# An MoE slot's layer 2 moved behind the next slot's layer 1, fetches without branches, late slots in two branches, weight regions at 64-byte multiples

## The chip, the core and the metric

The kernel runs on one core of a Trainium2 chip. The metric is the device time of one execution in microseconds; lower is better. Each kernel is executed several times and the median is given; one more execution is recorded by the hardware profiler, and all rows below come from that one.

## What is computed

A causal attention with a memory term, followed by a mixture of experts in which each token goes to its best expert. The reference, cut to what matters:

```python
# q, k, v: 4 batches, 8 heads, 576 positions, 64 columns, float32
a = softmax(causal(q @ k.T / 8));  local = a @ v
q_p = phi(q)                              # phi(x) = x + 1 for x > 0, exp(x) otherwise
mem = (q_p @ M_prev) / (q_p @ z_prev + 1e-6)
x = g * mem + (1 - g) * local             # g = 1 / (1 + exp(-beta)); then 2304 rows of 512
logits = normalised(x) @ normalised(expert_emb).T / tau      # 8 experts
e = argmax(logits);  gate = softmax(logits)[e]
for each expert e:                        # w1[e]: 512 x 1024, w2[e]: 1024 x 512
    out[rows of e] = gate * (relu(x @ w1[e]) @ w2[e])
```

## The kernel before

Until about 257 us the kernel computes the attention, then each token's expert; from then on the experts. The order of the first part is made by a small planner (`Sched`, lines 40 to 164): each operation has an engine, an assumed duration, dependencies and a priority, and the planner issues them by these. The table `PRIO` (line 37) holds the priorities' offsets; other numbers in it give another order of the same operations.

The expert stage works in slots of 128 rows, all of one expert. Three early slots, -3 to -1, belong to the expert with the most tokens and are planned together with the end of the attention (`early_slots`, line 1565). The main slots 0 to 24 follow in plainly written order (`l1`, `l2`, `first`, `second`, `rest`, from line 1645). Slots 0 to 14 always run (`NFIX` is 15). Each later one stands in a branch on a flag that the kernel computes (`when`, line 1636), nested in that of the slot before. With this data the slots 0 to 18 have rows, so slots 15 to 18 run inside branches, and 19 is the first that is skipped.

A slot's steps are:

- `off_reg`, `load_ids`, `gather`, `gather_g`: SyncE reads the slot's start from a table and loads its row numbers; GpSimd fetches the rows (L1422) and their gates (L1429) by indirect DMA. `x_T` is a transposing DMA on SyncE's queue (L1464) into one of two buffers `xT`; `x_hi` on ScalarE (L1468) and `x_lo` on VectorE (L1471) move its two halves to one of two places in `xhl`.
- Layer 1 (L1478): 4 chunks of 6 matmuls with 512 columns, three products of high and low parts for each half of the output, into two PSUM banks. `e_relu` (ScalarE, L1487) makes `hs`.
- `e_T` (L1491): 8 transposes of `hs` on TensorE. `e_hi` (ScalarE, L1495) and `e_lo` (VectorE, L1499) split the result into `hhl`.
- Layer 2 (L1505): 8 chunks of 3 matmuls with 512 columns. For a main slot `y_out` (VectorE, L1511) multiplies by the gate; for an early one `y_copy` (L1517) and a product on GpSimd (L1522) do that. `y_store` is an indirect DMA of GpSimd (L1529).

The weights come in fp32 into `RA` by DMA (L1340, L1342 for the early prefetch, L1351, L1354 later). Where a slot starts a new expert, `split_if` (L1437 is its branch) makes high and low parts on ScalarE (L1369) and VectorE (L1373), for layer 1 in `RB` and for layer 2 in `RC`. The matmuls of both layers read their 512 moving columns from `RB` and `RC`.

In the main stage the layers of neighbouring slots are woven together: half of layer 1 of slot i+1, its other half, half of layer 2 of slot i, the transposes of slot i+1, the other half of layer 2. Slot -1 isn't woven in: its layer 2 is finished in the early stage, before slot 0's layer 1. Slot 1's layer 1 takes slot 0's transposes in its middle (`if i == 1 and c == 1` in `l1`). In a branch each engine that takes part loads the flag and jumps for itself, and at the end of a branch not taken it makes up for the signals that it left out.

`pause` (line 226) is a tile of one element, allocated ahead of `RA`, `RB` and `RC`; in the built program these start at bytes 17,312, 50,080 and 82,848 of each partition, which is 32 bytes behind a multiple of 64.

Of the kernel before, what the change touches and what calls it, by code (L numbers as in the profile page):

```python
# [36 lines left out]
PRIO = {'po': {'S': -6.056184646814478, 'M': -5.666575449467843, 'E': 0.3840305535611125, 'T': -2.8418202194000335, 'H': -2.7510329935167688, 'L': -4.504325722743113, 'C': -0.7444419325520046}, 'pa': 0.08970844558892392, 'pv': -1.5671314454708472, 'sq': -14.84720101963438, 'xt': 2, 'ra': 0, 'aD': 1, 'ps': 1.7384297857956093, 'lv': 23.82858121560453, 'pr': 2.0466758035936374, 'rs': 0, 'w1p': 130.2350106796488, 'ag': 0, 'pb': 9.186065914959338, 'lqk': -2.2845849071912188, 'rr': 2, 'aA': 1, 'pe4': 2, 'ep': 143.81283877036086, 'w2p': 208.68596613061786, 'slack': 40.00092317974874, 'pp': 1.1250262799121031, 'fc': (1, 2), 'nw2l': 2, 'nw1l': 4, 'xlo': 1, 'wpd': 2, 'w1': 300000, 'ND': 2, 'avl': 2, 'ph': 1, 'avc': 1, 'phat': -11148.311932377628, 'ae': 1, 'rp': 0}  # L37
# [130 lines left out]
def kernel(  # L168
# [57 lines left out]
    pause = cst.tile([1, 1], F32, name="pause")  # L226
    gate_dram = dr.tile([NTOK + P, 1], F32, name="gate_dram")

# [3 lines left out]
    RC = cst.tile([P, 8192], F32R, name="RC")  # L232
    QK = [
# [1160 lines left out]
    G = {}  # L1394
# [153 lines left out]
    def early_slots():  # L1548
# [5 lines left out]
        for which in (1, 2):  # L1554
            for c in range(4):
                op(("wpf", which, c), "SP", 450,
                   lambda which=which, c=c: w_dma1(which, c, regs[-1]["nx"], cond=regs[-1]["pf"]),
                   (("wpr",), (f"w{which}l", c)) + ((), (("eix", 1),), (("exT", 0),), (("exT", 1),))[cfg.get("wpd", 2)], p0 + which, xfer=1456)
# [5 lines left out]
        for i in range(-NEARLY, 1):  # L1564
            pp = p0 + 10 * (i + NEARLY)
            old = i - 2 >= -NEARLY
            op(("exT", i), "SP", 1175, lambda i=i: x_T(i), (("eg", i),) + ((("gst",),) if i == 0 else ()) + ((("exs", i - 2), ("exl", i - 2)) if old else ()), pp, xfer=896)
            op(("exs", i), "ACT", c_act(512), lambda i=i: x_hi(i), (("exT", i),) + ((("el1", i - 2, KD - 1),) if old else ()), pp)
# [3 lines left out]
            for c in range(KD):  # L1572
                def f(i=i, c=c):
# [14 lines left out]
            op(("egg", i), "POOL", 1040, lambda i=i: gather_g(i), (("gst",), ("eix", i)), pp + 6, xfer=56, late=3500)  # L1588
            for c in range(KF):
                def f(i=i, c=c):  # L1590
                    if c == 0:
                        G[i]["yp"] = bank(("ey", i), "L" if i < -1 else "aux")
                    l2c(i, c)
                op(("el2", i, c), "PE", 3 * 236, f,
                   (("ehl", i, c // 4), ("w2l", c // 2)) + ((("el2", i, c - 1),) if c else ()), pp + 5,
                   alloc=() if c else (("L", ("ey", i)),) if i < -1 else (("aux", ("ey", i), 0, 3),))
# [45 lines left out]
    def maybe(i, engines):  # L1642
        return nullcontext() if i <= NFIX else when(i, engines)

    def l1(i):

        G[i]["hp"] = [pbank((2 if i == 1 else 0) + n) for n in range(2)]
        more = i + 1 < NSLOT
        for c in range(KD):
            l1c(i, c)  # L1650
            if i == 1 and c == 1:
                for n in range(2):
                    e_T(0, n, pbank(n))
                    e_hi(0, n)
                    e_lo(0, n)
        if more and i:
# [124 lines left out]
```

## Time and profile before

| | us |
|---|---|
| median of 3 runs | 556.67 |
| lowest and highest of them | 555.46 and 559.15 |
| the profiled execution | 553.01 |
| its span in the trace | 551.2 |

The mean granted clock of TensorE is 0.99 of its full speed in the profiled execution. Times in the rows count from the start of the span; the profiled execution's own time is 1.8 us longer than the span. PE is TensorE's matmuls, PEld its weight loads, which run beside them, DVE is VectorE, ACT ScalarE, POOL GpSimd and SP SyncE; a "q" behind a name is that engine's instruction queue, and a DMA that an engine issues stands under it. In rows of a timeline the first two numbers are the start and the duration, from the first instruction of the group to the end of the last; ends of matmuls are modelled and reach into the next group, so the pace is read from start to start. The square brackets give the idle time ahead of a group and what ended it.

### The profile page before, as it was taken

What the parts mean: (1) busy time and instruction counts of PE and PEld (TensorE: products, weight loads), DVE (VectorE), ACT (ScalarE), POOL (GpSimd) and SP (SyncE); (2) the same over time, 40 slices, a digit from 0 to 9 for tenths busy, and PEclk for the clock granted to TensorE, in tenths of its full rate; (3) what the DMA queues carried; (4) which work ended last, traced back from release to release, by engine and by line L of the source; (5) the groups of instructions that cost most, each with busy time, mean ns of one, the idle gap of its engine ahead of it and who ended that gap; (6) DMA issues with size and microseconds to landing.
All of it is one profiled execution on the core that took longest, in us unless ns stands there. A gap on an engine that the chain in (4) does not pass through costs nothing. (4 is left out here: it accounts for less than half of the span.)

```text
span 551.2 us, 11278 instructions
## 1 busy us (share of the span) xinstructions
PE 522.2 (95%) x3489; PEld 439.8 (80%) x3489; DVE 319.6 (58%) x1019; ACT 301.5 (55%) x592; POOL 226.3 (41%) x284
## 2 busy tenths in 40 slices
PE   7999999899999999998898899999999999999990
PEld 6788988798898989887686688888888888888870
DVE  5687777687777777789951133521267515664440
ACT  5777867676776867786322243422256525653340
POOL 6152573748446763777534322122232322212200
PEclk9999999999999999999999999999999999999996
DMA  6667744234643330579139636652268864774100
GB/s 156 138 82 161 178 92 117 48 73 108 156 91 45 77 65 14 124 246 168 39 66 357 110 75 232 161 96 58 59 211 278 222 170 122 245 235 156 39 15 21
DMA packets 124428, 70.33 MB, mean 128 GB/s; under 512 B 108600, under 2 KB 108728, under 8 KB 124354
## 3 DMA queue, kind: packets, MB, share of 16 engines
q1 hardware_dynamic: 119554, 58.96, 43.5%
q0 software_dynamic: 4800, 10.52, 6.7%
q8 instruction: 30, 0.49, 0.4%
q14 instruction: 44, 0.36, 0.2%
HBM read 110.69 MB, written 10.67 MB: 220 GB/s over the span
## 5 line engine op out<-in xcount | busy, mean ns | idle before, releaser
L1478 PE MATMUL aux<-RB,xhl 128*128 128x512 f32 x528 | 129.1, 398 | 2.8 <-ACTq L1437 2.8
L1505 PE MATMUL L<-RC,hhl 128*128 128x512 f32 x504 | 125.9, 399 | 0.3 <-ACT RC L1369 0.3
L1478 PEld LDWEIGHTS aux<-RB,xhl 128*128 128x128 f32 x528 | 98.8, 189 | 27.1 <-ACTq L1437 3.6
L1505 PEld LDWEIGHTS L<-RC,hhl 128*128 128x128 f32 x504 | 93.2, 188 | 21.9 <-issue 0.7
L1499 DVE TENSOR_TENSOR hhl<-aux,hhl 128x512 fp32r<-128x512 f32 x44 | 30.1, 689 | 117.0 <-ACT hhl L1495 54.7
L746 PE MATMUL L<-VN,aT 128*128 128x128 f32 x640 | 87.0, 276 | 0.0
L1529 POOL DMA_INDIRECT out_dram<-ys,ix x22 | 22.8, 1036 | 144.6 <-DVE ys L1511 130.1
L746 PEld LDWEIGHTS L<-VN,aT 128*128 128x128 f32 x640 | 78.4, 192 | 1.4 <-issue 0.6
L682 DVE CUSTOM_DVE_ANT_0 a<-aux,mask 128x128 f32<-128x128 f32 (+3 forms) x144 | 61.9, 452 | 14.0 <-PE aux L671 9.9
L1495 ACT ACTIVATE hhl<-aux 128x512 fp32r<-128x512 f32 x44 | 25.8, 595 | 74.2 <-PE aux L1491 43.9
L710 ACT ACTIVATE a<-a,nb 128x128 f32<-128x128 f32 (+3 forms) x128 | 65.1, 557 | 0.7 <-issue 0.2
L719 PE MATMUL aux<-ident,a 128*128 128x128 f32 x384 | 62.6, 280 | 1.6 <-ACT a L712 1.5
L731 ACT ACTIVATE aT<-aux 128x512 f32<-128x512 f32 (+3 forms) x83 | 42.4, 518 | 27.6 <-PE aux L719 26.2
L1487 ACT ACTIVATE hs<-aux 128x512 f32<-128x512 f32 x44 | 24.0, 595 | 55.4 <-PE aux L1478 55.1
L719 PEld LDWEIGHTS aux<-ident,a 128*128 128x128 f32 x384 | 42.7, 141 | 12.9 <-issue 4.0
L899 POOL TENSOR_TENSOR A<-ms,dd 128x256 f32<-128x256 f32 x32 | 20.5, 642 | 67.0 <-DVE dd L883 17.1
L1422 POOL DMA_INDIRECT a<-x_dram,ix x22 | 23.1, 1050 | 38.4 <-DMA ix<-id_dram 18.2
L1373 DVE TENSOR_TENSOR RB<-RA,RB 128x1024 fp32r<-128x1024 f32 x24 | 29.3, 1225 | 10.2 <-ACT RB L1369 10.2
L733 DVE COPY aT<-aux 128x512 f32<-128x512 f32 (+3 forms) x45 | 23.8, 530 | 12.4 <-PE aux L719 8.9
L649 POOL TENSOR_SCALAR RA<-RA 128x576 f32<-128x576 f32 x14 | 23.3, 1662 | 15.8 <-ACT RA L570 15.8
L1369 ACT ACTIVATE RB<-RA 128x1024 fp32r<-128x1024 f32 x24 | 25.4, 1061 | 7.0 <-PE aux L1478 6.3
L1373 DVE TENSOR_TENSOR RC<-RA,RC 128x1024 fp32r<-128x1024 f32 x24 | 27.8, 1220 | 1.5 <-ACT RC L1369 1.5
(252 smaller groups left out, 817.5 us busy)
## 6 DMA issues: line engine op xcount, KB each, us to landing
RA<-in_moe_w_dram SPq DMA_DIRECT2D x78, 1024.0 KB
RA<-in_moe_w_dram SPq DMA_DIRECT2D x16, 512.0 KB
RA<-in_k_dram SPq DMA_DIRECT2D x32, 128.0 KB
RA<-in_q_dram SPq DMA_DIRECT2D x32, 128.0 KB
VN<-in_v_dram SPq DMA_DIRECT2D x32, 128.0 KB
x_dram<-x SPq DMA_DIRECT2D x16, 256.0 KB
RA<-in_k_dram SPq DMA_DIRECT2D x8, 64.0 KB
RA<-in_q_dram SPq DMA_DIRECT2D x8, 64.0 KB
```

The source lines that it names most:

```text
L682: nc.vector.tensor_tensor_reduce(out=o, in0=i0, in1=i1, op0=ALU.add, op1=ALU.min, scale=-0.125, scalar=init, accum_out=acc)
L710: nc.scalar.activation(out=a[:, c], in_=a[:, c], func=AF.Exp, scale=-1.0, bias=nb[:, y : y + 1])
L719: nc.tensor.transpose(ps[:, P * y : P * y + P], a[:, P * y : P * y + P], ident)
L731: nc.scalar.activation(out=u["aT"][0:r, o : o + n], in_=t[0:r, 0:n], func=AF.Copy)
L746: nc.tensor.matmul(lt[:, P * hh : P * hh + P], u["aT"][:, P * y : P * y + P], vt[:, c : c + P], start=kb == 0, stop=kb == i)
L1369: nc.scalar.activation(out=h, in_=s, func=AF.Copy)
L1373: nc.vector.tensor_tensor(l, s, h.bitcast(F32), op=ALU.subtract)
L1478: nc.tensor.matmul(G[i]["hp"][n], a[:, cc], w[:, c, 512 * n : 512 * n + 512], start=c == 0 and a is xh and w is w1h, stop=c == KD - 1 and ...
L1487: nc.scalar.activation(out=G[i]["h"][:, 512 * n : 512 * n + 512], in_=G[i]["hp"][n], func=AF.Relu)
L1495: nc.scalar.activation(out=big("hhl")[n][:, 0:512], in_=G[i]["gps", n], func=AF.Copy)
L1499: nc.vector.tensor_tensor(t[:, 512:1024], G[i]["gps", n], t[:, 0:512].bitcast(F32), op=ALU.subtract)
L1505: nc.tensor.matmul(G[i]["yp"], t[:, cc : cc + P], w[:, c, :], start=c == 0 and a == 0 and w is w2h, stop=c == KF - 1 and a == 1)
```

## The change

1. Slot -1's layer 2 and what follows from it leaves `early_slots`. Its transposes, `e_hi` and `e_lo` now stand in `l1(0)` behind the second chunk, and `l2(-1, 0)` is woven with slot 0's as for all others; its output is written by `y_out`. Its layer 1 gets the fixed banks 4 and 5. `xT(1)` moves ahead of `l1(0)`, and `x_T(1)` and `x_T(2)` go into the planned part.
2. The fetches (`load_ids`, `gather`, `x_T`, `xT`, `gather_g`) of slots above 15 have no branch of their own any more.
3. A late slot has two branches instead of one with an Else: `first(i)`; then, outside of any branch of its own, `l2(i - 1, i)`; then `second(i)` and the next slot. For slot 19 the transposes and splits of a slot without rows are so executed inside slot 18's layer 2.
4. `pause` is allocated behind `RC`: the regions now start at bytes 17,280, 50,048 and 82,816, multiples of 64.
5. `PRIO` has new numbers for `po` (four of its seven), `lqk`, `lv`, `pv`, `sq`, `pr`, `ep`, `w1p`, `w2p`, `slack` and `phat`. `wpd` goes from 2 to 1 while the tuple that it picks from is shifted by one, so the prefetch still waits for the same transposing DMA.

```diff
-PRIO = {... 'ep': 143.81..., 'w1p': 130.23..., 'w2p': 208.68..., 'slack': 40.00..., 'wpd': 2 ...}
+PRIO = {... 'ep': 141.56..., 'w1p': 177.02..., 'w2p': 251.55..., 'slack': 37.70..., 'wpd': 1 ...}
-    pause = cst.tile([1, 1], F32, name="pause")
...
     RC = cst.tile([P, 8192], F32R, name="RC")
+    pause = cst.tile([1, 1], F32, name="pause")
...
-        for i in range(-NEARLY, 1):
-            pp = p0 + 10 * (i + NEARLY)
+        for i in range(-NEARLY, 3):
+            pp = p0 + 10 * (i + NEARLY) if i < 1 else p0
...
             op(("exT", i), "SP", 1175, lambda i=i: x_T(i), ...
+            if i > 0:
+                continue
...
-                   alloc=tuple(("aux", ("eh", i, n), 2) for n in range(2)) if c == 0 else ())
+                   alloc=() if c else tuple(("aux", ("eh", i, n), 0, 4 + n) for n in range(2)) if i == -1 else
+                   tuple(("aux", ("eh", i, n), 2) for n in range(2)))
             for n in range(2):
                 op(("ere", i, n), "ACT", c_act(512), lambda i=i, n=n: e_relu(i, n),
...
+                if i == -1:
+                    continue
...
             op(("egg", i), "POOL", 1040, lambda i=i: gather_g(i), (("gst",), ("eix", i)), pp + 6, xfer=56, late=3500)
+            if i == -1:
+                continue
...
     def l1(i):
-        G[i]["hp"] = [pbank((2 if i == 1 else 0) + n) for n in range(2)]
+        G[i]["hp"] = [pbank(n) for n in range(2)]
...
-            if i == 1 and c == 1:
+            if i == 0 and c == 1:
                 for n in range(2):
-                    e_T(0, n, pbank(n))
-                    e_hi(0, n)
-                    e_lo(0, n)
-        if more and i:
+                    e_T(-1, n, pbank(2 + n))
+                    e_hi(-1, n)
+                    e_lo(-1, n)
+        if more:
             split_if(i + 1, 1, range(KD - 1))
...
     def first(i):
-        if i == 0:
-            turn(1)
-            turn(2)
-        elif i + 1 < NSLOT:
-            with maybe(i + 1, CMP):
-                xT(i + 1)
+        if i + 1 < NSLOT:
+            xT(i + 1)
         if i + 4 < NSLOT:
-            fetch(i + 4)
-        if i and i + 3 < NSLOT:
-            turn(i + 3)
+            off_reg(i + 4)
+            load_ids(i + 4)
+            gather(i + 4)
+        if i + 3 < NSLOT:
+            x_T(i + 3)
...
     def rest(i):
...
-        with when(i, ALL) as go:
+        ch_reg(i)
+        pf_regs(i)
+        with when(i, ALL):
             first(i)
-            l2(i - 1, i)
+        l2(i - 1, i)
+        with when(i, ALL):
             second(i)
             rest(i + 1)
-        with go.Else():
-            l2(i - 1)
...
     for i in range(NFIX):
         first(i)
-        if i:
-            l2(i - 1, i)
-        else:
-            split_if(0, 2, range(4))
+        l2(i - 1, i)
         second(i)
```

TensorE's order where the early slots end and slot 0 begins, before (L1478 layer 1, L1491 transposes, L1505 layer 2, L256 matmuls that only keep the engine busy, L1437 the branch of `split_if`); the first L1478 row is slot -1's last chunk:

```order
L1505 MATMUL L<-RC,hhl 128x512 x24
L1478 MATMUL aux<-RB,xhl 128x512 x6
...
L1491 MATMUL aux<-ident,hs 128x128 x8
L1505 MATMUL aux<-RC,hhl 128x512 x24
L1437 UNCONDITIONAL_BRANCH
L1478 MATMUL aux<-RB,xhl 128x512 x24
L1437 UNCONDITIONAL_BRANCH x2
L1478 MATMUL aux<-RB,xhl 128x512 x12
L1491 MATMUL aux<-ident,hs 128x128 x8
```

And now (each line number is one higher):

```order
L1506 MATMUL L<-RC,hhl 128x512 x24
L1479 MATMUL aux<-RB,xhl 128x512 x6
L1438 UNCONDITIONAL_BRANCH
L1479 MATMUL aux<-RB,xhl 128x512 x12
L1492 MATMUL aux<-ident,hs 128x128 x8
L1479 MATMUL aux<-RB,xhl 128x512 x12
L1506 MATMUL L<-RC,hhl 128x512 x12
L1438 UNCONDITIONAL_BRANCH x2
L1492 MATMUL aux<-ident,hs 128x128 x8
```

Slot 0's layer 1 now follows slot -1's with a branch between; slot -1's transposes and its layer 2 come later, each beside matmuls of slot 0.

SyncE's queue at the same place, before (L1334 stores the gates, L1464 is the transposing DMA, L1340 the prefetch for layer 1, L1342 that for layer 2):

```order
L1334 DMA gate_dram<-g_178 128x18
L1464 DMA_TRANSPOSE xT_4246<-a 128x8x128
L1340 ISA
L1340 DMA RA<-in_moe_w_dram 128x1024
```

And now, where L1465 and L1341 are the same two:

```order
L1335 DMA gate_dram<-g_178 128x18
L1465 DMA_TRANSPOSE xT_4246<-a 128x8x128
L1465 DMA_TRANSPOSE xT_4247<-a 128x8x128
L1341 ISA
L1341 DMA RA<-in_moe_w_dram 128x1024
...
L1465 DMA_TRANSPOSE xT_4246<-a 128x8x128
L1341 ISA
L1341 DMA RA<-in_moe_w_dram 128x1024
L1343 ISA
```

Slot 1's transposing DMA now stands ahead of the prefetch, and slot 2's, which takes the buffer of slot 0's, ahead of the fourth piece of layer 1 and all of layer 2.

TensorE's order in the attention where the first matmuls with the memory stand, before (L719 transposes of the attention's weights, L746 these with V, L832 the memory `Mb`):

```order
L719 MATMUL aux<-ident,a 128x128 x4
L832 MATMUL aux<-Mb_88,qp_83 128x130 x4
L746 MATMUL L<-VN_85,aT 128x128 x4
```

And now:

```order
L747 MATMUL L<-VN_85,aT 128x128 x4
L833 MATMUL aux<-Mb_88,qp_83 128x130 x2
L720 MATMUL aux<-ident,a 128x128 x4
```

The four matmuls with V now stand ahead of the first ones with the memory, and the four transposes behind them. In the trace each matmul of L746 and L832 is two.

## Rows read from the trace of the kernel before

**Rows 1.** The page: engines; the costliest groups (busy, mean ns | idle, releaser).

```profile
PE 522.2 (95%) x3489; PEld 439.8 (80%) x3489; DVE 319.6 (58%) x1019; ACT 301.5 (55%) x592; POOL 226.3 (41%) x284
...
L1478 PE MATMUL aux<-RB,xhl 128*128 128x512 f32 x528 | 129.1, 398 | 2.8 <-ACTq L1437 2.8
L1505 PE MATMUL L<-RC,hhl 128*128 128x512 f32 x504 | 125.9, 399 | 0.3 <-ACT RC L1369 0.3
...
L1499 DVE TENSOR_TENSOR hhl<-aux,hhl 128x512 fp32r<-128x512 f32 x44 | 30.1, 689 | 117.0 <-ACT hhl L1495 54.7
...
L1495 ACT ACTIVATE hhl<-aux 128x512 fp32r<-128x512 f32 x44 | 25.8, 595 | 74.2 <-PE aux L1491 43.9
```

**Rows 2.** Windows: length, busy of each engine, PE clock, DMA share, GB/s.

```profile
0.00:257.00 257.00, 249.89 (x2199) 219.83 (x2199) 190.84 (x779) 187.33 (x423) 146.58 (x203) 1.00 0.51 112
...
325.00:500.00 175.00, 175.00 (x809) 142.62 (x808) 82.14 (x99) 79.49 (x112) 44.67 (x42) 1.00 0.60 173
```

**Rows 3.** Timeline of PE from the early slots' end to slot 2.

```profile
293.04 0.62 PE L256 MATMUL aux<-ident 128*128 128x128 f16 x8
294.81 1.14 PE L1491 MATMUL aux<-ident,hs 128*128 128x128 f32 x8 [1.15 <-ACT hs L1487]
297.47 5.87 PE L1505 MATMUL aux<-RC,hhl 128*128 128x512 f32 x24 [1.52 <-DVE hhl L1499]
304.40 5.88 PE L1478 MATMUL aux<-RB,xhl 128*128 128x512 f32 x24 [1.06 <-ACTq L1437]
311.98 3.07 PE L1478 MATMUL aux<-RB,xhl 128*128 128x512 f32 x12 [1.69 <-ACTq L1437]
314.88 1.04 PE L1491 MATMUL aux<-ident,hs 128*128 128x128 f32 x8
315.67 3.04 PE L1478 MATMUL aux<-RB,xhl 128*128 128x512 f32 x12
318.55 2.97 PE L1505 MATMUL L<-RC,hhl 128*128 128x512 f32 x12
321.36 1.04 PE L1491 MATMUL aux<-ident,hs 128*128 128x128 f32 x8
322.15 3.04 PE L1505 MATMUL L<-RC,hhl 128*128 128x512 f32 x12
325.03 5.78 PE L1478 MATMUL aux<-RB,xhl 128*128 128x512 f32 x24
```

**Rows 4.** Timeline of ACT around the same stretch.

```profile
294.17 1.07 ACT L1487 ACTIVATE hs<-aux 128x512 f32<-128x512 f32 x2
...
303.38 0.60 ACT L1517 ACTIVATE ys<-aux 128x512 f32<-128x512 f32 x1 [6.79 <-PE aux L1505]
...
326.69 1.06 ACT L1369 ACTIVATE RB<-RA 128x1024 fp32r<-128x1024 f32 x1 [0.57 <-PE aux L1478]
```

**Rows 5.** Timelines of SP and DVE in the same stretch.

```profile
286.50 1.28 SPq L1464 DMA_TRANSPOSE xT<-a  x1
...
291.63 3.01 SPq L1342 DMA_DIRECT2D RA<-in_moe_w_dram  x4
...
293.23 0.43 DVE L1471 CAST xhl<-xT 128x512 fp32r<-128x512 f16 x1 [6.60 <-DMA xT<-a]
```

**Rows 6.** Timeline of PE at the first matmuls with the memory.

```profile
17.82 1.13 PE L832 MATMUL aux<-Mb,qp 128*128 128x130 f32 x8 [1.26 <-DMA Mb<-in_z_prev_dram]
18.80 1.05 PE L746 MATMUL L<-VN,aT 128*128 128x128 f32 x8
```

**Rows 7.** Timelines of PE, DVE and POOL at the end.

```profile
531.18 6.03 PE L1505 MATMUL L<-RC,hhl 128*128 128x512 f32 x24 [0.29 <-ACT RC L1369]
...
537.31 0.75 DVE L1511 TENSOR_SCALAR ys<-L,gg 128x512 f32<-128x512 f32 x1 [2.09 <-PE L L1505]
...
541.24 1.01 POOL L1529 DMA_INDIRECT out_dram<-ys,ix  x1 [4.70 <-POOLq L1731]
```

**Rows 8.** Line L746 to 40 us: durations min/median/max in ns.

```profile
L746 PE MATMUL L<-VN,aT x79: 273/275/377, 13.4 to 39.9; 128*128 128x128 f32 x79
```

More of the change, by code (lines that the diff above doesn't have):

```diff
@@ L1557, in early_slots @@
                    lambda which=which, c=c: w_dma1(which, c, regs[-1]["nx"], cond=regs[-1]["pf"]),
-                   (("wpr",), (f"w{which}l", c)) + ((), (("eix", 1),), (("exT", 0),), (("exT", 1),))[cfg.get("wpd", 2)], p0 + which, xfer=1456)
+                   (("wpr",), (f"w{which}l", c)) + ((), (("exT", 0),), (("exT", 1),), (("exT", 2),))[cfg.get("wpd", 2)], p0 + which, xfer=1456)
         for i in range(4):
@@ L1591, in f @@
                     if c == 0:
-                        G[i]["yp"] = bank(("ey", i), "L" if i < -1 else "aux")
+                        G[i]["yp"] = bank(("ey", i), "L")
                     l2c(i, c)
@@ L1595, in early_slots @@
                    (("ehl", i, c // 4), ("w2l", c // 2)) + ((("el2", i, c - 1),) if c else ()), pp + 5,
-                   alloc=() if c else (("L", ("ey", i)),) if i < -1 else (("aux", ("ey", i), 0, 3),))
+                   alloc=() if c else (("L", ("ey", i)),))
             op(("ey", i), [("DVE", c_dve(512), lambda i=i: y_copy(i, "DVE")), ("ACT", c_act(512), lambda i=i: y_copy(i, "ACT"))],
@@ L1640, in when @@
         return tc.If(ACTIVE[key] > 0)
-    def maybe(i, engines):
-        return nullcontext() if i <= NFIX else when(i, engines)
     def l1(i):
-        G[i]["hp"] = [pbank((2 if i == 1 else 0) + n) for n in range(2)]
+        G[i]["hp"] = [pbank(n) for n in range(2)]
         more = i + 1 < NSLOT
@@ L1660, in l1 @@
         if more:
-            split_if(i + 1, 1, range(KD) if i == 0 else (KD - 1,))
+            split_if(i + 1, 1, (KD - 1,))
     def l2(i, n=None):
@@ L1682, in xT @@
         x_lo(i)
-    def fetch(i):
-        off_reg(i)
-        with maybe(i, SPP):
-            load_ids(i)
-            gather(i)
-    SPP = (ET.SP, ET.Pool)
-    CMP = (ET.Activation, ET.DVE)
     ALL = (ET.PE, ET.Activation, ET.DVE, ET.Pool, ET.SP)
-    def turn(i):
-        with maybe(i, (ET.SP,)):
-            x_T(i)
     def first(i):
-        if i == 0:
-            turn(1)
-            turn(2)
-        elif i + 1 < NSLOT:
-            with maybe(i + 1, CMP):
-                xT(i + 1)
-        if i + 4 < NSLOT:
-            fetch(i + 4)
-        if i and i + 3 < NSLOT:
-            turn(i + 3)
+        if i + 1 < NSLOT:
+            xT(i + 1)
+        if i + 4 < NSLOT:
+            off_reg(i + 4)
[3 more added lines that the diff above has]
+            x_T(i + 3)
         if i + 1 < NSLOT:
@@ L1713, in first @@
         l1(i)
-        if i == 0:
-            xT(1)
-            turn(3)
         if i + 1 < NSLOT:
@@ L1722, in second @@
         if i + 1 < NSLOT:
-            with maybe(i + 1, (ET.Pool,)):
-                gather_g(i + 1)
+            gather_g(i + 1)
     def rest(i):
```

2 lines of the change are left out of this document (1 added, 1 removed).

## The prediction

> **What bounds the kernel now.** I read the page's engine shares first, then the windows, then the costliest groups, and last the timelines around the places that the change touches. TensorE is busy for 522.2 of 551.2 us; no other engine passes 58% [rows 1]. So time can only come from TensorE's idle time (29 us in all), from its pace, or from what follows its last matmul. The windows say where the idle time is: from 325 to 500 us there is none, 175.00 busy of 175.00, and in the attention there are 7.1 us, 257.00 - 249.89 [rows 2]. The two groups of expert matmuls take 129.1 and 125.9 us, almost half of the span [rows 1], so their pace is the second thing to look at.
>
> **The transition (part 1).** Slot -1's layer 1 ends where the row of L256 begins, at 293.04, and slot 2 begins at 325.03: 31.99 us. The work in them is 96 matmuls with 512 columns (24 + 24 + 12 + 12 + 12 + 12) and three groups of 8 transposes [rows 3]. A matmul takes 0.2342 us from start to start, (321.36 - 318.55) / 12; 8 transposes take 0.79, 315.67 - 314.88 [rows 3]. That is 22.5 + 2.4 = 24.9 us of work, and 7.1 us are lost. The brackets name 1.15 + 1.52 + 1.06 + 1.69 = 5.4 of them: the chain relu, transposes, `e_hi`, `e_lo`, layer 2, in which nothing of another slot is woven, and two stops at ScalarE's queue. The rest is what the eight fill-in matmuls of L256 and the seams between groups cover.
>
> After the change slot 0's first layer needs no result of slot -1, only ScalarE's passing of the branch in front. ScalarE's relu ends at 294.17 + 1.07 = 295.24 [rows 4]. What the branch costs is shown once: ScalarE is done with its copy at 303.38 + 0.60 = 303.98 [rows 4] and the matmuls behind the branch start at 304.40 [rows 3], so 0.42. Slot 0 then starts at 295.66. The lost time is 295.66 - 293.04 = 2.6 us instead of 7.1, if the rest runs without gaps as the same pattern one slot later does (311.98 to 325.03 shows no bracket but its first [rows 3]). **-4.5 us**. Its bounds: -5.5 if the two ScalarE steps ahead of that relu (about 1 us) move behind it, and -3.4 if a stop at a branch such as the 1.06 us one comes back. The same 96 matmuls and 24 transposes are issued, so nothing else is removed on TensorE; the copy on ScalarE and two products on GpSimd lie beside other work, as both engines are under 56% busy [rows 1].
>
> What moves on SyncE's queue: slot 1's transposing DMA now stands ahead of all eight prefetches and slot 2's ahead of five of them. One takes 1.28 us of the queue [rows 5]. Slot 2's waits until slot 0's buffer has been read, at about 293.23 + 0.43 = 293.7 [rows 5]; five prefetches of 0.75 us (3.01 / 4) and its own 1.28 then end at about 298.7, against 294.6 before [rows 5]. The weights are first used at 326.69 [rows 4], 28 us later: no cost. Slot 1's rows are the delicate part: on ScalarE `x_hi(1)` stands ahead of `e_hi(-1)`, and waits for a transposing DMA that runs beside the prefetch. Slot 0's was issued at 286.50 and its reader started at 293.23, 6.7 us [rows 5]. The next one issues at 287.8. `e_hi(-1)` isn't needed before slot 0's layer 1 ends at 295.66 + 24 x 0.2342 + 0.79 = 302.1, less one `e_hi` and one `e_lo` (0.60 and 0.69 [rows 1]) and `x_hi` of about 0.6: the DMA may land as late as 300.2, 12.4 us after its issue, before it costs anything. I take nothing here, and keep its failing as a rival.
>
> **The attention (part 5).** The new priorities reorder only the attention. Its operations stay the same, and TensorE is at its pace in 97% of it [rows 2], so only its waits can change. One is visible in the reordered place: 1.26 us for the memory's DMA at 17.82 [rows 6]. Four program matmuls of L746 (eight in the trace, about 0.98 us by the eight from 17.82 to 18.80 [rows 6]) are put ahead of it, and four transposes (half of 0.79, 0.4 us) go behind it; 0.98 - 0.4 = about 0.5 of the wait is covered. **-0.5 us**. Bounds: -2.8 (the whole wait and a quarter of the other 5.8 us without work), and +1.5, if the new order opens one more wait of this size elsewhere.
>
> **Late slots and fetches (parts 2 and 3).** From 325 to 500 us TensorE has no idle time although slot 15 begins at 325.03 + 13 x 12.0 = 481 (a slot being 48 matmuls and 8 transposes, 12.0 us) and lies in a branch [rows 2, 3]. Its jumps are hidden in its instruction queue, and I cost the second branch and the missing ones of the fetches at nothing. What hides them is the queued work of TensorE; without this cover each join costs one wait of the size that the rows show for a stop at a branch, 1.06 to 1.69 us [rows 3]. At the end slot 18's layer 2 now has 8 transposes in it, +0.79. ScalarE's and VectorE's splits for the empty slot stand ahead of `y_out`; the first half runs beside the matmuls, and of the second, 0.60 + 0.69 us [rows 1], up to all is late. Data that was ready at 537.31 + 0.75 = 538.06 [rows 7] is then ready at 538.06 + 0.79 + 1.29 = 540.1. Before, the store waited on GpSimd's queue until 541.24, 3.2 us after its data; that idle time is ended by the queue's own L1731 [rows 7], the jump out of the nested branches. With the Else gone the store stands ahead of these jumps. It then starts at about 540.9, two thirds of a microsecond behind its data: **-0.3 us**, bounds -0.9 and +1.9.
>
> **Alignment (part 4).** The matmul's 234.2 ns stand against 213.3 for 512 columns at a column per cycle at 2.4 GHz, which is the level of the granted clock of 1.00 [rows 2]. So up to 20.9 ns could be lost in each, 22 us over the 528 + 504 + 24 of them [rows 1, 3]. Whether the start address is the reason no row shows, as every such matmul reads a region at 32 bytes behind a multiple of 64. The nearest row is L746: its blocks of V lie 65 values apart, so its starts take all multiples of 4 bytes, and yet 79 matmuls have a median of 275 ns with a least of 273 [rows 8]. But these have 128 columns and are bound by the weight load beside them. Bounds: -22 and 0; nothing excludes a loss, but I see no row for one. I take **0**, nearest to that row.
>
> The Trainium skill ("SBUF — State Buffer", section "Door 1: The DMA port swizzle") says that the memory is read in lines of 16 bytes and that an access pays when it crosses to a new one. Both the old and the new starts are multiples of 16, so by that rule nothing changes; the even durations of L746 [rows 8] don't contradict it. Another page ("TensorE: Matmul & The Clock Gate", section "Back-to-back issue gap") gives about 216 ns as the gap of a single matmul of this size; the trace's 234.2 is 18 above, and if that page's gap were reached the 1,056 matmuls would gain an estimated 19 us.
>
> **Sum.** -4.5 - 0.5 - 0.3 = -5.3 us. The profiled execution takes 553.01, 1.8 more than its span; it would take 547.7. It is 3.66 below the median of the runs shown, so the median becomes 556.67 - 5.3 = 551.4.
>
> **Rivals.**
>
> *The aligned regions quicken the matmuls.* For it: 20.9 ns per matmul are unexplained, and all of these matmuls are moved to the better address. Against: rows 8. Half of that gap would be 11 us, on top of the rest 540.4; a third, 7.4 us, gives 544. I take 543 for it.
>
> *Slot 1's rows come late.* The prefetch's eight issues follow at once; before, the last of them ended at 294.6 [rows 5] and slot 0's DMA took 6.7 us under them. If slot 1's needs 17 us, to 304.7, `e_hi(-1)` and with it layer 2 of slot -1 come 4.5 us late, and the gain of the transition is gone: 551.4 + 4.5 = 555.9. Against: 17 us is two and a half times the one that the rows show.
>
> *The joins of the late slots stop TensorE.* The slots 15 to 18 now have two branches each, with layer 2 of the slot before between them. If TensorE is held at each by an engine that has yet to make its jump, with the 1.69 us of the dearest stop in [rows 3], eight joins cost 13.5 us: 564.9. From 0.7 us a join the gain is gone. Against: the stretch with slot 15 has no idle time [rows 2], and the only stop near the end is 0.29 us [rows 7]. On the other side the Trainium skill ("Runtime: NRT & Kernel Launch", the paragraph on branches in "Instruction fetch mechanics") has a taken branch break the sequential fetch of instructions. By it each jump could stall; the trace's only such stop, 0.29 us, agrees at most weakly.
>
> *Something in the new order doesn't do what it says*, for instance a new wait in the attention at its bound of +1.5: 552.9, which lies in the forecast's own range.
>
> **How the numbers follow.** About 1% (5.6 us) is what a measurement of this kernel can tell from no change: faster means under 551.1, slower over 562.2. The forecast without an effect of the alignment (549 to 554) gets 0.50, and is split in the middle by that bound, 0.25 faster and 0.25 the same. The alignment gets 0.33, all of it faster. Slot 1's rows get 0.11: the same but for 0.01. The joins get 0.06, of which 0.05 is slower and 0.01 the same. Together faster 0.58, same 0.36, slower 0.06. The range goes from 540, the alignment's half gap, to 556.5, slot 1's rows late; the joins and the full gap of 22 us are left out.
>
> **What would show it.** In the profile after: slot 0's layer 1 should start about 2.6 us after slot -1's ends, layer 2 of slot -1 should follow it without a bracket, and slot 2 should begin 27.5 us after that end instead of 32.0. The wait for `Mb` should be about 0.7. From then on a slot should take 12.0 us, with 234 ns for a matmul; 215 to 230 would mean that the address counts. The last store should start about 0.3 us earlier against TensorE's last matmul of slot 18 than the transposes put it. Brackets of a microsecond in the slots 15 to 18, or a transposing DMA that lands after 300.2, would make it wrong on the slow side; a shorter start-to-start time of L1478's matmuls, on the fast side.

## The result and the profile after

The changed kernel takes 551.56 us (median of 17 runs, 547.58 to 558.39), the kernel before 555.46 beside it (17 runs, 553.37 to 559.19). The ratio is 0.9916, with a 95% interval of 0.9892 to 0.9941: 4.7 us faster, between 3.3 and 6.0. The profiled execution of the changed kernel took 552.41 us with a span of 550.7, so it lies 0.9 above its median, while that of before (553.01) lies 2.5 below the median of 555.46. The two profiles alone show only 0.5 us between the spans. I cut both spans at the same four places:

| stretch | before | after | difference |
|---|---|---|---|
| to the end of slot -1's layer 1 | 293.0 | 296.3 | +3.3 |
| from there to slot 2 | 32.0 | 26.3 | -5.7 |
| slot 2 to the end of the last matmul | 212.2 | 212.1 | -0.1 |
| from there to the end of the span | 14.0 | 16.0 | +2.0 |

The second row answers to [rows 3]. TensorE's timeline of the changed kernel there:

```profile
294.94 1.55 PE L1479 MATMUL aux<-RB,xhl 128*128 128x512 f32 x6
297.56 3.06 PE L1479 MATMUL aux<-RB,xhl 128*128 128x512 f32 x12 [1.06 <-ACTq L1438]
...
310.60 5.75 PE L1479 MATMUL aux<-RB,xhl 128*128 128x512 f32 x24
316.18 2.94 PE L1506 MATMUL L<-RC,hhl 128*128 128x512 f32 x12
...
322.64 5.75 PE L1479 MATMUL aux<-RB,xhl 128*128 128x512 f32 x24
```

Slot -1's layer 1 ends 6 x 0.234 us behind 294.94, at 296.34. One stop is left of the four in [rows 3], 1.06 us, and slot 2 begins 26.3 us later. The pace has changed as well: 24 matmuls take 5.58 us (316.18 - 310.60), 232.5 ns each, instead of 234.2.

The first row of the table is lost near 250 us. The same stretch in both timelines, first before (the V matmuls of the last row block are L754, the fourth chunk of slot -3's layer 1 is the last row):

```profile
252.10 1.58 PE L754 MATMUL L<-VN,aT 128*128 128x130 f32 x10 [0.71 <-ACT aT L731]
...
264.08 1.64 PE L1478 MATMUL aux<-RB,xhl 128*128 128x512 f32 x6
```

And after, where all line numbers are one higher:

```profile
252.64 2.83 PE L755 MATMUL L<-VN,aT 128*128 128x130 f32 x10 [3.12 <-ACT aT L732]
...
268.15 1.64 PE L1479 MATMUL aux<-RB,xhl 128*128 128x512 f32 x6
```

The same work takes 15.5 us instead of 12.0. The ten matmuls of the first row last 2.83 us instead of 1.58, and the windows say why (length, busy of PE, PEld, DVE, ACT and POOL, then the granted clock, DMA share and GB/s):

```profile
245.00:250.00 5.00, 4.52 (x42) 3.85 (x40) 2.87 (x8) 1.68 (x3) 4.40 (x6) 1.00 0.55 150
250.00:255.00 5.00, 2.36 (x9) 2.13 (x10) 3.75 (x10) 4.41 (x8) 4.74 (x6) 0.69 0.62 138
255.00:260.00 5.00, 4.53 (x18) 3.38 (x18) 1.77 (x4) 1.72 (x4) 1.71 (x2) 0.50 0.84 199
260.00:265.00 5.00, 5.00 (x32) 4.44 (x32) 4.06 (x15) 2.67 (x5) 1.52 (x1) 0.79 0.25 47
```

The same windows of the kernel before, for the second and third of these:

```profile
250.00:255.00 5.00, 3.66 (x27) 2.78 (x25) 4.50 (x14) 4.93 (x10) 4.75 (x5) 1.00 0.95 183
255.00:260.00 5.00, 4.91 (x37) 4.16 (x38) 4.77 (x14) 3.17 (x6) 2.22 (x3) 1.00 1.23 188
```

Around and behind a stop of 3.12 us the granted clock is at 0.50, its lower level of 1.2 GHz, and comes back within the fourth window. Before, the stop was 0.71 us and the clock 1.00 throughout. Who TensorE waited for is read on ScalarE and GpSimd, in the changed kernel:

```profile
250.44 0.63 ACT L942 ACTIVATE x<-X 128x512 f32<-128x512 f32 x1 [3.75 <-POOL X L906]
...
252.01 0.73 ACT L732 ACTIVATE aT<-aux 128x512 f32<-128x512 f32 x2
...
249.67 0.73 POOL L906 TENSOR_TENSOR X<-A,Xl 128x256 f32<-128x256 f32 x1
```

The copy L732 stands in ScalarE's queue behind a sum of squares (L942), and that one stood 3.75 us for a block that GpSimd had not added up. So the row of PE names ScalarE, but GpSimd was late. Whether this belongs to the change was the first question for the runs.

The end answers to [rows 7]:

```profile
531.68 3.05 PE L1506 MATMUL L<-RC,hhl 128*128 128x512 f32 x12
...
535.82 0.74 DVE L1512 TENSOR_SCALAR ys<-L,gg 128x512 f32<-128x512 f32 x1
...
536.84 1.03 POOL L1530 DMA_INDIRECT out_dram<-ys,ix  x1 [2.39 <-DVEq L1723]
```

The last store starts 2.1 us behind the last matmul's end (534.73) instead of 4.0, and yet the span ends 2.0 us later relative to it: 12.8 us lie behind the store (537.87 to 550.7) instead of 9.0. GpSimd's own instructions on L1723, the second branch of the late slots, between 530 and 551 us:

```profile
L1723 POOLq EVENT_SEMAPHORE  x5: 17/43/2797, 537.1 to 537.4; - x5
...
L1723 POOLq INC_SWDGE_SEM  x1: 1950/1950/1950, 540.3 to 540.3; - x1
```

And those of the kernel before on its branch, L1731, between 530 and 552 us:

```profile
L1731 POOLq EVENT_SEMAPHORE  x4: 17/43/43, 541.0 to 541.3; - x4
...
L1731 POOLq INC_SWDGE_SEM  x1: 1856/1856/1856, 541.4 to 541.4; - x1
```

Where the branch isn't taken, GpSimd makes up for the signals of what it skips. The longest of its waits there, 2.8 us, is on the semaphore of the store that it has just issued; one step more takes 1.95 us, and only then does it reach the program's end. Before, the step stood behind the store as well, with 1.86 us, so it is no new cost. The wait is new: none of GpSimd's waits there passed 43 ns before, as it issued the store at the end of its way out of the branches, and the wait for the store was SyncE's.

### The profile page after: what moved, and what is told of

It reads as the page before. It is cut to its first block, busy times and chain, and to the rows that moved or that the text cites. A ratio compares the mean times of both kernels' runs of the same rounds, so it can differ in the third digit from the quotient of the medians.

```text
span 550.7 us, 11324 instructions
## 1 busy us (share of the span) xinstructions
PE 523.8 (95%) x3489; PEld 443.1 (80%) x3489; DVE 321.3 (58%) x1022; ACT 303.8 (55%) x595; POOL 231.4 (42%) x288
## 5 line engine op out<-in xcount | busy, mean ns | idle before, releaser
L1506 PE MATMUL L<-RC,hhl 128*128 128x512 f32 x528 | 131.5, 398 | 0.4 <-ACT RC L1370 0.4
L1506 PEld LDWEIGHTS L<-RC,hhl 128*128 128x128 f32 x528 | 97.7, 188 | 22.5 <-ACT RC L1370 0.8
L1500 DVE TENSOR_TENSOR hhl<-aux,hhl 128x512 fp32r<-128x512 f32 x46 | 31.5, 689 | 126.1 <-ACT hhl L1496 65.7
L1496 ACT ACTIVATE hhl<-aux 128x512 fp32r<-128x512 f32 x46 | 27.1, 595 | 82.8 <-PE aux L1492 47.5
L732 ACT ACTIVATE aT<-aux 128x512 f32<-128x512 f32 (+3 forms) x85 | 44.3, 528 | 29.4 <-PE aux L720 28.6
L1488 ACT ACTIVATE hs<-aux 128x512 f32<-128x512 f32 x44 | 24.0, 595 | 51.6 <-PE aux L1479 51.3
L1423 POOL DMA_INDIRECT a<-x_dram,ix x26 | 28.4, 1094 | 48.8 <-DMA ix<-id_dram 23.8
L755 PE MATMUL L<-VN,aT 128*128 128x130 f32 (+1 forms) x160 | 26.4, 307 | 3.6 <-ACT aT L732 3.6
```

Of the source, the lines that this page charges most:

```text
L732: nc.scalar.activation(out=u["aT"][0:r, o : o + n], in_=t[0:r, 0:n], func=AF.Copy)
L755: nc.tensor.matmul(lt[:, P * hh : P * hh + 2 * (D + 1)], u["aT"][0:r, P * kb : P * kb + P], vn[0:r, kb, hh : hh + 2, :].rearrange("p h e - ...
L1423: nc.gpsimd.indirect_dma_start(out=xg, out_offset=None, in_=x_dram[0:rows, :], in_offset=bass.IndirectOffsetOnAxis(ap=ix[:, 0:1].bitcast(U ...
L1496: nc.scalar.activation(out=big("hhl")[n][:, 0:512], in_=G[i]["gps", n], func=AF.Copy)
L1500: nc.vector.tensor_tensor(t[:, 512:1024], G[i]["gps", n], t[:, 0:512].bitcast(F32), op=ALU.subtract)
L1506: nc.tensor.matmul(G[i]["yp"], t[:, cc : cc + P], w[:, c, :], start=c == 0 and a == 0 and w is w2h, stop=c == KF - 1 and a == 1)
```

## The experiments

**Theory A**, from the account above: part 1 takes 5.7 us out of the transition; the second branch costs 2 us at the end and 0.8 for the transposes of an empty slot; the address is worth 1.7 us of pace; the new order of the attention gains nothing, and its stop with the fall of the clock costs a few us wherever it happens. **Theory B** is the forecast's own terms: -4.5, -0.3, 0 and -0.5. **Theory C**: the address carries most of the gain.

Twelve kernels ran in three groups, each group on one chip with runs of the kernel before beside it, so a ratio is taken to that group's own before (medians 557.29, 561.66 and 557.70 us).

**Part 1 alone.** The kernel before with slot -1's layer 2 moved, and nothing else.

```diff
+                if i == -1:
+                    continue
...
-            if i == 1 and c == 1:
+            if i == 0 and c == 1:
```

> The kernel before with part 1 alone: slot -1's layer 2 behind slot 0's layer 1; old priorities, old branches, pause ahead of the regions. Theory A (the account from the two profiles): the stretch from the end of slot -1's layer 1 to slot 2 takes 26.3 us instead of 32.0, so 5.7 us faster than before (ratio 0.990), with the end as before (about 14 us from TensorE's last matmul to the end of the span) and 234 ns a matmul. Theory B (the forecast's terms): 4.5 us faster (0.992). Theory C (the change gains by something else): at most 2 us faster.

Measured: 553.44 us, ratio 0.9940 (0.9912 to 0.9969), 3.3 us faster, between 1.7 and 4.9. Its TensorE:

```profile
296.75 1.56 PE L1479 MATMUL aux<-RB,xhl 128*128 128x512 f32 x6
300.40 4.61 PE L1479 MATMUL aux<-RB,xhl 128*128 128x512 f32 x12 [2.08 <-ACTq L1438]
...
327.11 5.78 PE L1479 MATMUL aux<-RB,xhl 128*128 128x512 f32 x24
```

The stretch takes 29.0 us (298.16 to 327.11), not 26.3, with a stop of 2.08 us at slot 0's first matmul. Part 1 gains what the forecast gave it, within this interval; 5.7 was the size in one execution. C's 2 us at most lie near the end of the interval. The stop near 250 us is here too, 3.1 us long, in the old order.

**The old priorities in the changed kernel.**

```diff
-PRIO = {... 'ep': 141.56..., 'w1p': 177.02..., 'slack': 37.70..., 'wpd': 1 ...}
+PRIO = {... 'ep': 143.81..., 'w1p': 130.23..., 'slack': 40.00..., 'wpd': 1 ...}
```

> The changed kernel with the old priorities, so with the attention's old order. Theory A: the new order gains 1.9 us until 249 us, GpSimd takes it back, and the stop of 3.1 us that is left makes the granted clock fall to half for 10 us; without it the clock stays at 1.00 around 252 to 262 us and the time is 1 to 4 us below the changed kernel's, by how many of its executions have the fall: 5.4 us below before. Theory B: 0.5 us above the changed kernel, as the new order covers half a microsecond of a wait.

Measured: 554.52 us, ratio 0.9938 (0.9906 to 0.9969). Against the changed kernel's 0.9916 and 0.9906 (below) that is about 1.5 us slower, with an uncertainty of some 2. The stop near 250 us is 3.1 us with the old order as well:

```profile
254.58 2.60 PE L755 MATMUL L<-VN,aT 128*128 128x130 f32 x10 [3.11 <-ACT aT L732]
```

So theory A is wrong in this point: neither the stop nor the fall of the clock belongs to the new order. B's half microsecond fits, but can't be told from nothing. (This edit takes back every number of part 5; of `po` five of the seven had changed, not four.)

**Late slots in one branch again.**

```diff
-        with when(i, ALL):
+        with when(i, ALL) as go:
             first(i)
-        l2(i - 1, i)
-        with when(i, ALL):
+            l2(i - 1, i)
             second(i)
             rest(i + 1)
+        with go.Else():
+            l2(i - 1)
```

> The changed kernel with a late slot in one branch with an Else again. Theory A: 14.0 us instead of 16.0 from TensorE's last matmul to the end of the span, so 2 us below the changed kernel (and 0.8 for the transposes that slot 19 no longer has), about 0.995 of it. Theory B: 0.3 us above the changed kernel, as the store stands behind the jumps again.

Measured: 551.84 us, ratio 0.9919 (0.9884 to 0.9953). The end of its profile (span 545.9):

```profile
526.51 5.92 PE L1506 MATMUL L<-RC,hhl 128*128 128x512 f32 x24 [0.41 <-ACT RC L1370]
...
535.37 1.04 POOL L1530 DMA_INDIRECT out_dram<-ys,ix  x1 [2.29 <-POOLq L1720]
```

From the last matmul's end (532.43) to the span's end are 13.4 us, 2.6 fewer than in the changed kernel, although the store starts 2.9 us behind that matmul instead of 2.1. All six profiles with two branches have the wait for the store, 2.5 to 3.0 us, and none of the eight with one branch has it. The mechanism is shown; in the ratio it isn't seen, as 0.0035 on either side is 2 us.

**pause ahead of the regions again.**

```diff
+    pause = cst.tile([1, 1], F32, name="pause")
...
     RC = cst.tile([P, 8192], F32R, name="RC")
-    pause = cst.tile([1, 1], F32, name="pause")
```

> The changed kernel with pause ahead of the regions again, so these at 32 bytes behind a multiple of 64. Theory A: 234.0 ns a matmul instead of 232.4 from start to start, 1.7 us above the changed kernel (1.003). Theory B: no difference, 232.4 ns is not due to the address. Theory C (the alignment carries most of the gain): 4 us above.

Measured: 555.89 us, ratio 0.9973 (0.9943 to 1.0003), 0.6% above the changed kernel's 0.9916: about 3 us, with an uncertainty of some 2. TensorE's timeline of it:

```profile
296.60 1.56 PE L1479 MATMUL aux<-RB,xhl 128*128 128x512 f32 x6
301.39 4.60 PE L1479 MATMUL aux<-RB,xhl 128*128 128x512 f32 x12 [3.23 <-ACTq L1438]
...
328.09 5.78 PE L1479 MATMUL aux<-RB,xhl 128*128 128x512 f32 x24
333.71 1.57 PE L1506 MATMUL L<-RC,hhl 128*128 128x512 f32 x6
```

The pace is back at 234.2 ns (5.62 / 24). Theory B's zero is refuted. But slot 0's stop is 3.23 us here, and the twelve matmuls behind it last 4.60 us instead of 3.06: the clock fell at this place too. The address moves no instruction, so what makes that stop longer or shorter has to be found elsewhere:

```profile
291.32 4.23 SPq L1465 DMA_TRANSPOSE xT<-a  x2
...
299.69 0.43 DVE L1472 CAST xhl<-xT 128x512 fp32r<-128x512 f16 x1 [7.89 <-DMA xT<-a]
```

Slot 0's transposing DMA needs 8.4 us from its issue to its reader. In the changed kernel's profile it was 5.2:

```profile
289.50 3.07 SPq L1465 DMA_TRANSPOSE xT<-a  x2
...
294.71 0.43 DVE L1472 CAST xhl<-xT 128x512 fp32r<-128x512 f16 x1 [4.55 <-DMA xT<-a]
```

ScalarE reads these rows (`x_hi`, L1469) ahead of slot -1's relu (L1488) and of the branch. First its row here, then the rows of the changed kernel:

```profile
299.69 0.63 ACT L1469 ACTIVATE xhl<-xT 128x512 fp32r<-128x512 f16 x1 [2.29 <-DMA xT<-a]
```

```profile
295.63 0.62 ACT L1469 ACTIVATE xhl<-xT 128x512 fp32r<-128x512 f16 x1
296.31 1.08 ACT L1488 ACTIVATE hs<-aux 128x512 f32<-128x512 f32 x2
```

Here the stop at "ACTq" is this DMA. In the changed kernel's profile it is not: `x_hi` has no bracket there, and the stop of 1.06 us is the relu, which ends at 297.39, and the branch behind it, 0.17 us.

**The changed kernel once more**, with no edit, for a second profile.

> The changed kernel as it is, once more, beside the three below. Theory A: 0.9916 of before as measured; a second profile has the stop near 250 us at the ScalarE copy L732 again, the fall of the granted clock behind it, and a stop of 1 to 4 us at slot 0's first matmul whose length follows the landing of slot 0's transposing DMA. Rival (the stop near 250 us belongs to the one profiled execution alone): under 1 us there, clock 1.00 from 252 to 270 us.

Measured: 555.03 us, ratio 0.9906 (0.9874 to 0.9938), the same as at first. The stop near 250 us is 2.2 us long and the clock 0.50 from 255 to 260; slot 0's stop is 2.0 us with 5.8 for the DMA.

```profile
253.60 2.28 PE L755 MATMUL L<-VN,aT 128*128 128x130 f32 x10 [2.22 <-ACT aT L732]
```

```profile
297.28 0.62 ACT L1469 ACTIVATE xhl<-xT 128x512 fp32r<-128x512 f16 x1
```

The rival falls. Theory A holds for the stop near 250 us, but not for slot 0's: `x_hi` has no bracket in this profile either, so ScalarE found its rows in place. It came to them late itself, for a reason that the rows don't show.

**Fill-in matmuls in the stop near 250 us.**

```diff
             hh = u["hs"][0]
+            if gi == gl and u["x"] == 0:
+                for _ in range(24):
+                    nc.tensor.matmul(lt[:, P * hh : P * hh + P], ident16, ident16, start=True, stop=True)
```

> The changed kernel with 24 small matmuls of the identity with itself (results overwritten at once) ahead of the last row block's matmuls with V whose input is late, where TensorE stood 3.1 us. They take about 1.9 us of the stop. Theory A (the stop makes the clock fall): the granted clock from 252 to 262 us is 1.00 instead of 0.50, matmuls there take half the time, about 3 us below the changed kernel where that has the fall, 1 to 3 in the median. Rival (the work behind the stop waits for GpSimd's and VectorE's chain to the expert table anyway): no gain; the stops behind it grow by what is saved.

Measured: 554.77 us, ratio 0.9882 (0.9835 to 0.9930), no difference that the intervals tell from 0.9906. In its profile the stop was longer, 2.8 us behind the fill-in, and the clock was 0.71 from 255 to 260 and 0.95 in the next five. The mean granted clock of its runs rose from 0.981 to 0.986, but the stop at the expert table (L1065 waiting for `roh`) grew from 0.5 to 2.0 us. Both theories hold a part: the clock falls less, and VectorE's chain to the table takes much of it back.

**One branch, and fill-in matmuls at both stops.** As above with the Else, and 16 more ahead of slot 0's layer 1.

```diff
+        if i == 0:
+            for _ in range(16):
+                nc.tensor.matmul(G[i]["hp"][0][:, 0:P], ident16, ident16, start=True, stop=True)
```

> The changed kernel with one branch and an Else for late slots, the 24 fill-in matmuls near 250 us and 16 more ahead of slot 0's layer 1. Theory A: 2.0 us from the end, 1 to 3 from the clock: 3 to 5 us below the changed kernel, 0.983 of before. Rival: only the end, 2 us below (0.988).

Measured: 551.95 us, ratio 0.9849 (0.9811 to 0.9887), 8.5 us below before and 3.5 below the changed kernel's mean of 0.9911, with an uncertainty of some 2.5: what theory A gave, and the rival's 2 us aren't excluded. Its windows:

```profile
250.00:255.00 5.00, 4.08 (x47) 3.61 (x45) 2.90 (x15) 2.97 (x7) 4.79 (x6) 1.00 0.49 115
255.00:260.00 5.00, 4.29 (x35) 3.24 (x34) 4.90 (x7) 3.28 (x7) 4.17 (x3) 1.00 1.08 187
260.00:265.00 5.00, 5.00 (x36) 4.15 (x36) 4.77 (x12) 3.45 (x8) 2.43 (x1) 1.00 0.53 131
265.00:270.00 5.00, 2.98 (x24) 2.37 (x23) 4.97 (x18) 2.38 (x4) 2.40 (x1) 1.00 0.15 54
270.00:275.00 5.00, 4.94 (x35) 3.82 (x32) 2.94 (x24) 0.64 (x2) 2.98 (x5) 0.66 0.24 53
```

The clock stays at 1.00 where the fill-in stands, and falls behind the next stop, that of 2.0 us at the expert table.

**Part 4 alone.** The kernel before with pause behind the regions.

```diff
-    pause = cst.tile([1, 1], F32, name="pause")
...
     RC = cst.tile([P, 8192], F32R, name="RC")
+    pause = cst.tile([1, 1], F32, name="pause")
```

> The kernel before with part 4 alone: pause behind the regions. Theory A: 232.4 ns a matmul instead of 234.0, 1.7 us below before (0.997). Theory B (no effect of the address): 234.0 and no difference. Theory C: 4 us below (0.993).

Measured: 558.59 us, ratio 0.9939 (0.9909 to 0.9968), 3.4 us faster, between 1.8 and 5.1. TensorE's timeline, and below it the row of its waits for the stop near 250 us:

```profile
331.78 5.75 PE L1478 MATMUL aux<-RB,xhl 128*128 128x512 f32 x24
337.37 2.94 PE L1505 MATMUL L<-RC,hhl 128*128 128x512 f32 x12
```

```profile
PE L L754 <- ACT aT L731: 3.6, 2, 3.1
```

24 matmuls take 5.59 us, 232.9 ns by these rounded starts. The mean over all such starts behind 325 us in layers 1 and 2 is 232.3 and 232.6 here, 232.2 and 232.6 in the changed kernel, and 234.3 and 233.7 in the kernel before. The address is worth 1.1 to 2.0 ns a matmul, 1.7 us over 1,056. The ratio's middle is twice that, and 1.7 lies just outside its interval; by time alone theory C isn't excluded, it is the pace that speaks against it. The granted clock may hold the rest: it is 0.982 on the mean of these runs and 0.979 of those of before beside them. That is an estimated 3.7 us less at 0.50, in which up to 1.9 us of work is lost. Whether the address has a part in this or chance alone, no run shows. The stop of 3.1 us stands here in the kernel before but for an address: the profile before had happened on an execution without it.

**The prefetch behind slot 2's transposing DMA.**

```diff
-PRIO = {... 'wpd': 1 ...}
+PRIO = {... 'wpd': 3 ...}
```

> The changed kernel with all eight pieces of the weights' prefetch behind slot 2's transposing DMA on SyncE's queue, so that they start only when slot 0's has been read. Theory A2 (the stop at slot 0's first matmul is as long as slot 0's transposing DMA is late, and the prefetch issued right behind it slows that): 5.2 us or less from its issue to its reader, where the changed kernel and its variants showed 5.2 to 8.4; a stop of about 1 us instead of 1.1 to 3.7; 26.3 us or less from slot -1's layer 1 to slot 2; 1 to 2 us below the changed kernel (0.988 of before). Rival (the DMA waits on something else, such as its issue or the gathers): the same 5 to 8 us and no difference.

Measured: 553.86 us, ratio 0.9926 (0.9893 to 0.9959). Its SyncE, VectorE and TensorE:

```profile
291.96 8.70 SPq L1465 DMA_TRANSPOSE xT<-a  x3
...
296.96 0.43 DVE L1472 CAST xhl<-xT 128x512 fp32r<-128x512 f16 x1 [4.47 <-DMA xT<-a]
...
300.43 3.05 PE L1479 MATMUL aux<-RB,xhl 128*128 128x512 f32 x12 [1.79 <-ACTq L1438]
```

```profile
298.73 0.62 ACT L1469 ACTIVATE xhl<-xT 128x512 fp32r<-128x512 f16 x1
```

The DMA takes 5.0 us. In this and the three profiles below it took 4.8 to 5.3; with the prefetch right behind it, in eight profiles, 4.9 to 8.9, 6.5 on the mean. The stretch to slot 2 is 26.7 to 27.0 us in all four, against 26.3 to 30.5 (28.4 on the mean) in the eight. ScalarE stood at `x_hi` for the DMA in five of the eight, with stops of 1.8 to 3.7 us at slot 0's first matmul, and in none of the four. This fits a collision with the prefetch; but the four are this last group's, on a chip on which no experiment has the early prefetch, so the chip isn't excluded. Theory A2's stop of about 1 us did not come: it is 1.79 us, although the rows were there. So the DMA makes the long stops, and ScalarE's own steps ahead of the branch make one of 1.1 to 2.0 us without it. That an end of the collision would make the kernel faster was not seen, as 0.9926 lies no lower than 0.9911, the mean of the changed kernel's two.

**The same with one branch.** The edit with the Else and that of the prefetch together.

> As the one before, with one branch and an Else for late slots. Theory A: 2.0 to 2.5 us less from TensorE's last matmul to the end and 0.8 for slot 19's transposes, so 0.995 of the one before. Theory B (what e3's time suggested, whose ratio did not differ from the changed kernel's): no difference, the jumps with an Else cost in the slots what the end gains.

Measured: 551.70 us, ratio 0.9896 (0.9859 to 0.9934), 1.7 us below the one before, with an uncertainty of about 2.8. From the last matmul to the end it takes 13.2 us, 15.8 in the one before. Nothing in the slots gives it back: from slot 2 to the last matmul's end are 211.4 us, 212.1 with two branches.

**The same with both fill-ins.**

> As the one before, with the 24 and 16 fill-in matmuls. Theory A: the granted clock doesn't fall near 255 us in most executions; 1 to 2 us less, 0.980 of before. Rival: no difference, as the next stop at the expert table takes it back.

Measured: 550.41 us, ratio 0.9896 (0.9866 to 0.9926): no difference, though the clock is 1.00 from 250 to 270 us in its profile. The stop at the expert table is 2.0 us, 1.5 in the one before; the rival holds.

**The sum of squares behind the copy.** In place of the 24 fill-in matmuls.

```diff
+        if key == (3, 2):
+            deps = deps + (("P", units[-2]["n"], 0), ("P", units[-2]["n"], 1))
         op(("sq", key), "ACT", 816, sq, deps, p0, ...
```

> As the one before, but in place of the 24 fill-in matmuls the sum of squares of the last but two blocks (ScalarE, L942), which waits for GpSimd, is put behind the copy L732 that TensorE waits for; the planner moves a few more operations with it. Theory A2 (TensorE's stop near 250 us is ScalarE standing at that sum in its queue): the stop is under 1 us and the granted clock stays at 1.00 there; 0.5 to 2 us less than with the fill-in matmuls. Rival (the copy waits for its own input): the stop stays at 2 to 3 us.

Measured: 548.03 us, ratio 0.9837 (0.9804 to 0.9870), 9.1 us below before and 3.3 below the one before it, with an uncertainty of some 2.5: the best version of all, though not separated from the 0.9849 above. Its profiled execution took 554.64 us, well above its median, so near 250 us only its order of events is used:

```profile
254.12 1.58 PE L755 MATMUL L<-VN,aT 128*128 128x130 f32 x10
...
259.44 0.44 PE L987 MATMUL aux<-ident,X 128*128 128x128 f32 x2 [1.37 <-POOL X L906]
```

The stop at the copy is gone: L755 has no bracket. TensorE now waits directly for GpSimd's sum, 1.4 us, and for VectorE's, 2.0, some microseconds later. It was ScalarE standing in line, and behind that GpSimd. The clock stays at 1.00 from 250 to 265 us, and falls behind VectorE's stop: it is 0.50 from 270 to 275.

## Why the prediction was right, and where it was not

The time was right: 551.4 foretold, 551.56 measured; -5.3 us foretold, -4.7 measured (3.3 to 6.0). That the two times agree to 0.2 us is luck: the forecast started from 556.67, the median of three runs, and 17 have 555.46. By its own bound (faster means under 551.1) the change came out as the same, to which it had given 0.36, and not as faster, which had 0.58. By its terms:

**The transition, -4.5.** Right in mechanism and, as far as these profiles tell, in size. In the first pair of profiles it is -5.7, just beyond the bound of -5.5. Eight profiles with part 1 and the early prefetch have 28.4 us on the mean, two without part 1 have 32.0 and 33.3: -4.2. By time, part 1 alone is 3.3 us faster. I took the stop that is left from the relu's end and 0.42 us for the branch, and that is what it is in the changed kernel's two profiles, 1.1 and 2.0 us. What the sum had not seen is a second cause: slot 0's own transposing DMA, which ScalarE reads first. In five of the eight it was late, and the stop 1.8 to 3.7 us. The rival "slot 1's rows come late" had the DMA under the prefetch right and the slot wrong: slot 1's never stopped TensorE, as no bracket stands at layer 2 of slot -1 in any of these timelines.

**The attention, -0.5.** Not told from zero. The wait for `Mb` is gone from TensorE's waits, but not by the order alone: with the old priorities in the changed kernel it is gone too, and a profile with the new order has 0.6 us of it. The start of the last four matmuls with the memory, the last place ahead of the stop near 250 us, is at 250.95 us on the mean of four profiles with the old order (250.73 to 251.19), and at 250.81 of nine with the new (248.86 to 252.18). What the new order wins early is within what executions differ by.

**Late slots, -0.3.** This step failed: "With the Else gone the store stands ahead of these jumps." It does, and starts 1.9 us earlier relative to the last matmul, but I let the span's end follow the store. It follows GpSimd's queue, which now passes the branch not taken with its store still under way. From the last matmul to the end are 15.7 to 16.1 us in six profiles with two branches, and 13.2 to 14.0 in eight with one: 2.3 us on the mean (2.0 against the three that have the fetches' branches as well), above my bound of +1.9 for the whole step. The transposes of slot 19 cost 0.9 more: from slot 2 to the last matmul's end are 212.1 us with aligned regions and 213.1 without, and with an Else 211.2 and 212.2. Together +3.2. Part 2 has no run of its own, but with one branch and aligned regions this stretch is 211.2 us with the fetches' branches (part 4 alone) and 211.2 without them: no cost, as forecast. The rival of joins that stop TensorE in the slots 15 to 18 did not come: 325 to 500 us are 175.00 busy, as in [rows 2], and 500 to 525 us 25.00. The stop of 0.29 us that the rival took for one at a jump has ScalarE's split of `RC` in its bracket [rows 7]; it is 0.40 in the changed kernel.

**The address, 0.** Wrong by a small amount: the 512-column matmuls go from 234.0 to 232.4 ns, 1.6 of the 20.9 ns that I gave as the most. By this pace it is -1.7 us for all 1,056. From slot 2 to the last matmul, with 840 of them, the stretch is 1.0 us shorter, which would make 1.3 for all. The row that I leaned on, [rows 8], has matmuls with 128 columns and couldn't show it. I had drawn from the lines of 16 bytes in the Trainium skill ("SBUF — State Buffer", section "Door 1: The DMA port swizzle") that two starts at multiples of 16 are alike; that does not hold for this row: the measurement decides. The new starts are multiples of 128 as well as of 64, so no run shows which of the two counts. The rival's 11 us, half the gap, did not come.

So two errors met: 3 us lost at the end, 1.3 to 1.7 won by the address. The measured terms add up to -4.2 - 1.7 + 3.2 - 0.1 = -2.8 us (-2.4 to -3.1 by which of these figures are taken), against -4.7 (3.3 to 6.0), so that some 2 us of the gain have no term, and the total came out better than its parts. The ratios of single parts would give more for the address (-3.4, and about -3 in the test that takes it back). Whether it is worth more than the pace shows, or these ratios lie at the edge of their intervals by chance, stays open. So does what decides in which executions GpSimd is late near 250 us.

## What to carry to other kernels

Read the profiled execution's place among the runs before summing from it: this one had missed a stop, and a fall of the clock behind it, that all nine later profiles of kernels without a remedy had. Its granted clock of 0.99 was a sign: the 75 runs of the same kernel beside the experiments have 0.981 on the mean and 0.988 at most. A wait on an engine's queue is a question, not an answer; go back on that engine to the first instruction that stood for something (a sum on GpSimd near 250 us, and in five profiles a DMA at slot 0), and ask it again in a second profile, as the answer can differ. And what follows the last store counts: an engine that must still wait for a DMA to pass a branch sets the end, not the DMA's start.

## What the runs showed of the hardware that was not expected

- The same matmuls with 512 fp32r columns take 234.0 ns from start to start with the moving operand at 32 bytes behind a multiple of 64, and 232.4 at a multiple of 128; that held for layers 1 and 2 in every profile of either kind (three and eleven).
- TensorE stopped for 2.0 to 3.7 us at 23 places of the fourteen profiles. At 20 of them the granted clock fell to 0.50 late in the stop or within 2 us behind it, and stayed there for 3 to 10 us; in the changed kernel's profile that made 12.0 us of work into 15.5. At the other three, of 2.0 us each, it stayed at 1.00.
- GpSimd, passing a branch not taken with an indirect store under way, stood 2.5 to 3.0 us for that store in six profiles. The step behind it, 1.95 us, takes as long without the wait (1.86 to 1.96).
- A transposing DMA took 4.8 to 5.3 us from issue to reader with no prefetch behind it in the queue (four profiles), and 4.9 to 8.9 with three weight transfers issued behind it before it was read (eight, on other chips).
